# A planned attention-and-MLP kernel: lock rules for the port of VectorE and GpSimd, and a fourth quad with twenty VectorE tiles

## The chip, the cores and the metric

The kernel runs on one core of a Trainium2 chip. A core has TensorE (PE, matrix products), ScalarE (ACT, the exponential), VectorE (DVE), GpSimd (POOL) and a sync engine (SP) that issues DMAs. Each engine works through its own list of instructions in order; semaphores hold one engine back for another. Matrix products land in PSUM, eight banks of 128 x 512 float32; everything else lies in SBUF. The metric is device time in microseconds (us) for one execution, as the median over runs.

## The reference

One sequence of 2048 rows, width 512, in bfloat16. Attention with 32 heads of 16 channels, and a bilinear MLP with 1376 hidden channels, both on the same input, are mixed by a gate of each row:

```python
def _A_ref(x, wqkv, wo):                 # H = 32, Dh = 16
    qkv = (x @ wqkv).reshape(B, S, 3, H, Dh).transpose(2, 0, 3, 1, 4)
    q, k, v = qkv[0], qkv[1], qkv[2]
    scores = jnp.einsum("bhqd,bhkd->bhqk", q, k) * (Dh ** -0.5)
    p = softmax(scores, axis=-1)
    o = jnp.einsum("bhqk,bhkd->bhqd", p, v)
    return o.transpose(0, 2, 1, 3).reshape(B, S, D) @ wo
...
    h = jnp.einsum("bsd,df->bsf", x, w_gate) * jnp.einsum("bsd,df->bsf", x, w_up)
    b = jnp.einsum("bsf,fd->bsd", h, w_down)
...
x = A_x
g = sigmoid((x * gate_w).sum(-1, keepdims=True))
return g * a + (1 - g) * b
```

There are 32 heads x 2048 x 2048 scores, and each needs an exponential.

## The kernel before

**Tiles and quads.** Queries are cut into four chunks of 512. A *quad* is one chunk and four heads; there are 8 quads in a chunk and 32 in all, numbered m = 0 to 31. A *tile* is 128 keys by 512 queries of one head, so a quad has 16 key blocks x 4 heads = 64 tiles. TensorE makes a tile's scores with 32 of its rows, so up to four tiles of a quad are made at once (line 488, one step of `run_scores`).

**Two ways to the exponential.** Most tiles go to ScalarE: one instruction of `act_step` (line 1689) takes two or three neighbouring PSUM banks and writes bfloat16 into as many *cells* (512 columns of SBUF; most are in `PT`, others in `wv`, `hT` and `wd` while these are free). The other tiles, *D tiles*, go to VectorE (line 1076), which adds a constant to the scaled score, clips and stores it as a 16-bit integer that is read as bfloat16. This rough exponential is refined by averaging: three further copies of it with 32, 64 and 96 added (lines 1154 on VectorE, 1157 on GpSimd, made by `try_copy`, two tiles or on VectorE sometimes four at a time) are multiplied with weighted copies of V (`VD`, made on GpSimd at line 704; `VE`, line 718). A ScalarE tile thus needs one product with V, a D tile four (line 1219, `do_pv`, all into the bank psO).

**The split.** In an ordinary quad 48 tiles go to ScalarE and 16 to VectorE. For the quads in `HBQ` four more are D tiles (`xd`, with the key blocks in `XU`), 44 and 20. The extra ones need the small copies in `VE`, made for each block of 8 heads that occurs in `HBQ`. After a quad, psO is copied to SBUF (line 1248), reciprocals of the sums go through DRAM (SP's DMAs), and GpSimd multiplies (line 1280).

**Banks.** Six PSUM banks (psS) form two slots of three for scores. The first two of a slot always take ScalarE tiles; the third takes a ScalarE tile or a D tile. A seventh, psX, takes D tiles and *fills*: everything that is not attention (projections of Q, K and V, the MLP's up, gate and down products, the output product), as groups of up to 11 packs of four matmuls. VectorE evicts each fill. A Q fill is evicted to `qtmp` (line 622) and from there copied twice with a mask into `QM` (line 632), SBUF to SBUF.

**The planner.** The order on every engine is written by a simulation in `_build` that runs when the program is built. It keeps a clock for each engine, and steps the engine whose clock is lowest. Each task has a planned duration (`occ`) and a priority; `gen_step` picks for VectorE and GpSimd, `pe_step` and `filler` for TensorE, `act_step` for ScalarE. A fill has a position, in ScalarE tiles issued (`st["ua"]`), from which on it may run; `F0`, `F1`, `HWF` and `warp` set the positions of the MLP's fills. Only the order and the semaphores go into the program; on the chip an engine goes as fast as it is let.

**The lock.** [...] The plan keeps `lock["dve"]` and `lock["pool"]`, the times until which each holds it. GpSimd takes nothing before `lock["dve"]`; VectorE takes no weight copy (`try_copy`) before `lock["pool"]`; and a GpSimd task gets as dependency the VectorE task in front of the last weight copy (`lock["op"]`), so that the copy gets to the port first. The Q copies of line 632 are planned with 0.22 us and are outside of this rule:

```python
            if eng == "pool" and t < lock["dve"]:
                clock[eng] = lock["dve"]
                return True
```

Of the kernel before, what the change touches and what calls it, by code (L numbers as in the profile page):

```python
# [112 lines left out]

class _Task:

    __slots__ = ("eng", "deps", "fn", "occ", "lat", "prio", "cb", "stream", "dma", "op", "start", "end", "alloc", "pre")

    def __init__(self, eng, deps, fn, occ, lat=None, prio=5, cb=None, stream=None, dma=False, alloc=None):
        self.eng = eng
        self.deps = [d for d in deps if d is not None]  # L120
        self.fn = fn
        self.occ = occ
        self.lat = occ + 0.13 if lat is None else lat
        self.prio = prio
        self.cb = cb
        self.stream = stream
        self.dma = dma
        self.op = None
        self.start = None
        self.end = None  # L130
        self.alloc = alloc
        self.pre = None


class _Cell:
# [61 lines left out]
def _build(nc, A_x, A_wqkv, A_wo, W_gate, W_up, W_down, gate_w, out):  # L197
# [18 lines left out]
    NM = NQ * NCH  # L216
    RA = 24
    VW = 18
    HBQ = [16, 24, 30]
    HB = sorted({(m % NQ) // 2 for m in HBQ})  # L220
    XU = {1: 3, 4: 2, 7: 1, 10: 0}
    XI = {1: 0, 4: 1, 7: 2, 10: 3}
# [12 lines left out]
    with ExitStack() as stack:  # L235
# [243 lines left out]
            return old  # L479

        PACK = 0.2135
        PLAT = 0.44
        SW = 0.11
        pe = {"mode": "c"}
# [119 lines left out]
        def f_q(c, b, pos):  # L604
            packs = [
                (
                    lambda bk, kt=kt: col(
                        bk.ap, wq[:, kt, b * 128 : (b + 1) * 128], xT[:, kt, c * 512 : (c + 1) * 512], kt == 0, kt == KD - 1
                    ),
                    PACK,  # L610
                    "c",
                )
                for kt in range(KD)
            ]

            def evac(bk, last):
                if QT and (c or b):
                    bk.need += 1
                    e0 = add(
                        "dve",  # L620
                        [last] + qt_last,
                        lambda v: v.tensor_single_scalar(qtmp[:], bk.ap, QS, ALU.mult),
                        0.6,
                        prio=2,
                        cb=lambda k: bk.readers.append(k),
                    )
                    qt_last.clear()
                    for p in range(2):
                        ev_q[c, b, p] = add(
                            "dve",  # L630
                            [e0, o_mask] + q_last.get((c - 1, b), []),
                            lambda v, p=p: v.tensor_scalar(QM[:, p, b, :], qtmp[:], mask[:, p : p + 1], None, ALU.mult),
                            0.22,
                            prio=3.2,
                        )
                        qt_last.append(ev_q[c, b, p])
                    return
                bk.need += 2
                for p in range(2):
                    ev_q[c, b, p] = add(  # L640
                        "dve",
                        [last, o_mask] + q_last.get((c - 1, b), []),
                        lambda v, p=p: v.tensor_scalar(QM[:, p, b, :], bk.ap, mask[:, p : p + 1], QS, ALU.mult, ALU.mult),
                        0.66,
                        prio=2,
                        cb=lambda k: bk.readers.append(k),
                    )

            def deps():
                if c and not q_done.get((c - 1, b)):  # L650
                    return [None]
                return [d_wq[b]] + xdep(c)

            return Fill(f"q{c}{b}", packs, deps, evac, pos)
# [445 lines left out]
        def try_copy(eng, t):  # L1100
            best = None
            if eng == "pool" and dve_busy(t) < PB:
                return None
            for i, pr in enumerate(pairs):
                if not pr["k"] or not full(pr):
                    continue
                r = max(k.end for k in pr["p1"]) + (0.0 if eng == "dve" else SEM)
                if r > t:
                    continue
                if eng == "pool":  # L1110
                    k = pr["k"][-1]
                    if k < PK:
                        continue
                else:
                    k = pr["k"][0]
                    if k == 3 and r + (0.5 if st["ua"] >= NA - 12 else KW) > t:
                        continue
                best = (pr, k)
                break
            if best is None:  # L1120
                return None
            pr, k = best
            prs_ = [pr]
            if eng == "dve" and M4 and len(pr["u"]) == 2:
                for p2 in pairs[i + 1 : i + 4]:
                    if k in p2["k"] and full(p2) and len(p2["u"]) == 2 and max(x.end for x in p2["p1"]) <= t:
                        if even(pr["cell"] + p2["cell"]):
                            c = alloc(4, t)
                            if c is not None:
                                prs_.append(p2)  # L1130
                                break
            us = [(p_, x) for p_ in prs_ for x in range(len(p_["u"]))]
            n = len(us)
            c = alloc(max(n, 2), t)
            if c is None:
                return None
            c = c[:n]
            old = claim(c, 1)
            for p_ in prs_:
                p_["k"].remove(k)  # L1140
                if not p_["k"]:
                    pairs.remove(p_)
            if n == 4:
                _build.m4 += 1

            def cb(tk):
                for i, (p_, x) in enumerate(us):
                    cells[p_["cell"][x]].readers.append(tk)
                    add_tile(*p_["u"][x], k, c[i], tk)

            I16 = mybir.dt.int16
            src = tuple(p_["cell"][x] for p_, x in us)
            if eng == "dve":
                fn = lambda v: v.tensor_single_scalar(cell_ap(c, I16), cell_ap(src, I16), 32.0 * k, ALU.add)  # L1154
                occ = DCP + 0.133 * n
            else:
                fn = lambda g: g.tensor_scalar(cell_ap(c, I16), cell_ap(src, I16), 32.0 * k, 1.0, ALU.add, ALU.mult)  # L1157
                occ = PCP + 0.435 * n
            return _Task(eng, [x for p_ in prs_ for x in p_["p1"]] + old, fn, occ, cb=cb)
# [151 lines left out]
        QO = [0, 3, 1, 4, 2, 5, 6, 7]  # L1311
        fills = [q0[i] for i in QO] + q0[8:]
        wts = []
        HWF = 0.3
        GP = 200.0
        K3L = 190
        K3H = 260
# [9 lines left out]
        F0 = 210.0  # L1327
        WP = 36.0
        WL = 18.0
        F1 = 1490.0  # L1330
        fills.append(f_gate(GP))
        HW = 44.0 * HWF

# [103 lines left out]
        PB = 0.45  # L1437
        PK = 2
        KW = 4.0
        LAP = 0.1  # L1440
        LAC = 0.1
        CPR = 3.5
        LC = 6
        LDO = 8
        MG = 0.15
        FLATE = 12
# [4 lines left out]
        LA1 = 1  # L1451
        LA2 = 99
        XF = -99
        FB = 2
        SWE = 0
        NFD = 18
        AOH = 0.057
        M4 = 1
        _build.m4 = 0
# [1 line left out]
        PCP = 0.14  # L1461
        DEV = 0.6
        RSV = 0.5
        NP = 8
        KP = 1
        FBL = 15

        def a_idx():
# [231 lines left out]
        def gen_step(eng):  # L1700
            t = clock[eng]
            best = None
            if eng == "pool" and t < lock["dve"]:
                clock[eng] = lock["dve"]
                return True
            for k in qs[eng]:
                if best is not None and k.prio >= best.prio:
                    continue
                r = ready(k)
                if r is not None and r <= t:  # L1710
                    if k.alloc is not None:
                        old = k.alloc(t)
                        if old is None:
                            WHY.append((t, "p1cell"))
                            continue
                        k.deps = k.deps + old
                        k.alloc = None
                    best = k
# [4 lines left out]
            if eng in ("dve", "pool") and (best is None or best.prio > CPR):  # L1723
                if eng == "pool" or lock["pool"] <= t:
                    c = try_copy(eng, t)
                    if c is not None:
                        if eng == "dve":
                            lock["op"] = lock["prev"]
                            lock["prev"] = c
                        elif lock["op"] is not None:  # L1730
                            c.deps.append(lock["op"])
                        run_task(c, t)
                        lock[eng] = clock[eng]
                        return True
            if best is None:
                return False
# [1 line left out]
            if eng == "pool" and lock["op"] is not None:  # L1738
                best.deps.append(lock["op"])
            run_task(best, t)  # L1740
            if eng == "dve":
                lock["prev"] = best
            if eng == "pool":
                lock["pool"] = clock["pool"]
            return True

        o_woz = add(
# [208 lines left out]
```

The softmax here doesn't subtract the row's maximum and nothing guards it: scores larger than these inputs give would overflow.

## Time and profile before

| | |
|---|---|
| median of 3 runs | 714.72 us (714.56 to 714.99) |
| profiled execution, its own time | 714.88 us |
| span in that profile | 713.1 us |
| granted TensorE clock | 1.00 |
| first exponential starts, last one starts | 9.13 us, 702.74 us |
| instructions on line 1689 | 674 |

The page gives the busy time of each engine as a share of the span. A group row names line, engine, operation, output and input with shapes, the count, then busy time, mean duration in ns, and the idle time of the engine just before, with what ended it. In the order of time a row gives start, duration and count. ScalarE's instructions overlap in the records: a following one starts before the recorded end of the one before it, so durations are longer than the distance from start to start.

### The profile page before, as it was taken

To read this page: it belongs to the slowest core of one execution; us is meant where nothing else is said; L and a number is where in the kernel's file an instruction comes from. 1 tells how busy PE (TensorE), PEld (TensorE's weight loads), DVE (VectorE), ACT (ScalarE), POOL (GpSimd) and SP (SyncE) were. 2 spreads that over 40 slices of the span, in tenths; PEclk is the share of its full clock that TensorE was granted. 3 is DMA by queue.
4 is the path that set the end of the run, shared out by engine and by line. 5 is a ranking of instruction groups with operands and counts; after the bars stand their busy time and mean duration, and the time that the engine had idled before them with its cause. 6 is when DMAs were issued, how large, how long until landed. Compare 5 with 4: busy or idle time off the path is not lost. (4 is left out here: it accounts for less than half of the span.)

```text
span 713.1 us, 21304 instructions
## 1 busy us (share of the span) xinstructions
PE 688.0 (96%) x9115; PEld 188.2 (26%) x9115; DVE 643.2 (90%) x1229; ACT 699.1 (98%) x689; POOL 439.2 (62%) x463
## 2 busy tenths in 40 slices
PE   8999999999999999999999999999999999999997
PEld 3323232222222222222222222222222222222222
DVE  5999989999999888899988888999889988999887
ACT  6999999999999999999999999999999999999995
POOL 4648676565656566576577566655557676555682
PEclk9999999999999999999999999999999999999999
DMA  7700001000200001000000010000000000000001
GB/s 142 255 12 9 21 18 19 19 17 22 81 20 18 17 16 32 26 17 17 20 3 28 17 44 25 18 13 10 21 18 17 18 28 29 17 21 18 3 20 46
DMA packets 33055, 21.65 MB, mean 30 GB/s; under 512 B 20381, under 2 KB 27965, under 8 KB 32961
## 3 DMA queue, kind: packets, MB, share of 16 engines
q1 hardware_dynamic: 31632, 19.64, 9.2%
q8 instruction: 71, 1.16, 0.7%
q10 hardware_dynamic: 1328, 0.66, 0.4%
q14 instruction: 24, 0.19, 0.1%
HBM read 15.12 MB, written 2.36 MB: 25 GB/s over the span
## 5 line engine op out<-in xcount | busy, mean ns | idle before, releaser
L1689 ACT ACTIVATE PT<-psS 128x1024 bf16<-128x1024 f32 (+1 forms) x577 | 625.9, 1420 | 0.7 <-PE psS L488 0.6
L1157 POOL TENSOR_SCALAR PT<-PT 128x1024 int16<-128x1024 int16 x220 | 237.0, 1086 | 146.1 <-DVE PT L1154 38.9
L488 PE MATMUL psS<-QM,KE 32*128 32x512 bf16 x1968 | 255.2, 376 | 12.3 <-ACT PT L1689 6.6
L1076 DVE TENSOR_SCALAR PT<-psS 128x512 int16<-128x512 f32 x328 | 221.8, 685 | 23.9 <-PE psS L488 20.2
L1219 PE MATMUL psO<-PT,VS 128*18 128x512 bf16 x1709 | 227.7, 381 | 0.7 <-DVE oraw L1248 0.6
L1219 PE MATMUL psO<-PT,VD 128*18 128x512 bf16 x1231 | 192.3, 381 | 0.1
L1017 PEld LDWEIGHTS <-KE 32*128 32x128 bf16 x2048 | 63.1, 91 | 279.4 <-issue 166.4
L1154 DVE TENSOR_SCALAR PT<-PT 128x1024 int16<-128x1024 int16 (+1 forms) x232 | 101.4, 466 | 2.1 <-PE psO L1219 0.8
L1157 POOL TENSOR_SCALAR PT<-wv 128x1024 int16<-128x1024 int16 x57 | 61.0, 1078 | 40.9 <-DVE wv L1076 16.5
L1219 PEld LDWEIGHTS psO<-PT,VS 128*18 128x18 bf16 x1709 | 52.2, 88 | 59.8 <-issue 42.4
L1689 ACT ACTIVATE wv<-psS 128x1024 bf16<-128x1024 f32 (+1 forms) x47 | 60.3, 1311 | 0.0
L557 PE MATMUL psX<-wd,hT 128*32 128x512 bf16 (+1 forms) x704 | 59.0, 386 | 0.3 <-DVE wk L867 0.3
L1076 DVE TENSOR_SCALAR wv<-psS 128x512 int16<-128x512 f32 x76 | 51.8, 686 | 6.8 <-PE psS L488 6.3
L1219 PEld LDWEIGHTS psO<-PT,VD 128*18 128x18 bf16 x1231 | 45.3, 88 | 36.4 <-issue 22.9
L557 PE MATMUL psX<-xT,wu 128*32 128x512 bf16 x688 | 53.2, 383 | 1.0 <-DVE wv L1076 0.7
L557 PE MATMUL psX<-xT,wg 128*32 128x512 bf16 x688 | 52.5, 383 | 1.0 <-DVE PT L1076 0.7
L1219 PE MATMUL psO<-wv,VS 128*18 128x512 bf16 x182 | 49.9, 381 | 0.5 <-DVE oraw L1248 0.5
L1076 DVE TENSOR_SCALAR PT<-psX 128x512 int16<-128x512 f32 x58 | 39.8, 686 | 6.6 <-PE psS L488 6.4
L1689 ACT ACTIVATE wd<-psS 128x1024 bf16<-128x1024 f32 (+1 forms) x35 | 42.0, 1289 | 0.0
L1219 PE MATMUL psO<-wv,VD 128*18 128x512 bf16 x167 | 38.2, 381 | 0.0
L1157 POOL TENSOR_SCALAR wv<-PT 128x1024 int16<-128x1024 int16 x24 | 25.6, 1068 | 20.3 <-PE psO L1219 10.0
L830 DVE TENSOR_TENSOR hT<-psX,usb 128x512 bf16<-128x512 f32 (+1 forms) x44 | 30.0, 682 | 4.4 <-PE psX L557 4.3
(127 smaller groups left out, 704.0 us busy)
## 6 DMA issues: line engine op xcount, KB each, us to landing
rb<-rscr SPq DMA_DIRECT2D x31, 256.0 KB
out_dram<-ost SPq DMA_DIRECT2D x12, 128.0 KB, 1.7
wu<-in_B_w_up_dram SPq DMA_DIRECT2D x1, 1376.0 KB, 10.1
wg<-in_B_w_gate_dram SPq DMA_DIRECT2D x1, 1376.0 KB, 13.0
wd<-in_B_w_down_dram SPq DMA_DIRECT2D x1, 1280.0 KB, 6.1
OT<-OX SPq DMA_DIRECT2D x60, 16.0 KB, 1.8
wo<-in_A_wo_dram SPq DMA_DIRECT2D x1, 512.0 KB, 13.0
out_dram<-wk SPq DMA_DIRECT2D x4, 128.0 KB, 1.7
```

Source lines behind the costliest of these rows:

```text
L488: return e.add_instruction(mybir.InstMatmult(name=nc.get_next_instruction_name(), engine=mybir.EngineType.PE, ins=[e.lower_ap(rhs), e.lowe ...
L557: return e.matmul(out_ap[32 * q : 32 * q + w, :], lhs[:, 32 * q : 32 * q + w], rhs, start=s0, stop=s1, tile_position=(0, 32 * q), skip_gro ...
L830: lambda v: v.tensor_tensor(hT[0:w, f, :], bk.ap[0:w, :], usb[0:w, n % 2, :], ALU.mult),
L1017: r = e.ldweights(w, tile_position=pos)
L1076: lambda v: v.tensor_scalar(cell_ap(pr["cell"][i : i + 1], mybir.dt.int16), bk.ap, CB, 0.0, ALU.add, ALU.max),
L1154: fn = lambda v: v.tensor_single_scalar(cell_ap(c, I16), cell_ap(src, I16), 32.0 * k, ALU.add)
L1157: fn = lambda g: g.tensor_scalar(cell_ap(c, I16), cell_ap(src, I16), 32.0 * k, 1.0, ALU.add, ALU.mult)
L1219: r = e.matmul(psO[32 * j : 32 * j + VW, :], pv_stationary(m, kt, j, k), cell_ap((cell,)), start=s0, stop=s1, tile_position=(0, 32 * j), s ...
L1689: lambda a: a.activation(cell_ap(c), src, ACT.Exp, scale=LN2 / 128.0),
```

## The change

- `HBQ` becomes [16, 22, 24, 30]: quad 22 also gets 20 D tiles and 44 ScalarE tiles. The set of head blocks with `VE` copies stays {0, 3}.
- Tasks get a flag `x4`; the Q copies of line 632 carry it, and their planned duration goes from 0.22 to 0.26 us. A flagged task is not taken while GpSimd holds the port; taking it sets VectorE's lock and `lock["op"]`. GpSimd takes nothing while VectorE is within 0.3 us (`QMW`) of being free with a flagged task ready by then.
- GpSimd may start 0.07 us before the end of VectorE's lock (`LKD`); GpSimd's lock ends 0.1 us before its planned end (`LKP`).
- `try_copy` asks for a reserve of free cells (`RSC`) for copies of a quad later than the one whose products with V are running: two for each copy still owed to tiles up to the running quad. The reserve that the eviction of a D tile asks for is cut to three quarters (`KP`).
- Positions of the MLP's fills: `HWF` 0.3 to 0.2, `F1` 1490 to 1460. Their end goes from 1438.4 + 3 x 13.2 = 1478 to 1408.8 + 4 x 8.8 = 1444.
- Planner's numbers: `LAP` 0.1 to 0.12 (how long VectorE waits for a D tile that is about to be ready), `LC` 6 to 7 (how far D tiles may lag before one is converted to ScalarE), `FB` 2 to 0 (fills may start up to the time of the next scores), `NFD` 18 to 20 (free cells below which products with V go before a down product).

```diff
@@
-    __slots__ = (..., "alloc", "pre")
+    __slots__ = (..., "alloc", "pre", "x4")
...
-    HBQ = [16, 24, 30]
+    HBQ = [16, 22, 24, 30]
...
         PACK = 0.2135
+        QMC = 0.26
+        LKD = -0.07
+        LKP = 0.1
+        QMP = 3.2
+        QMW = 0.3
...
                             lambda v, p=p: v.tensor_scalar(QM[:, p, b, :], qtmp[:], mask[:, p : p + 1], None, ALU.mult),
-                            0.22,
-                            prio=3.2,
+                            QMC,
+                            prio=QMP,
+                            x4=True,
                         )
...
-            c = alloc(max(n, 2), t)
+            c = alloc(max(n, 2), t, False, RSC * sum(len(x["k"]) for x in pairs if x["u"][0][0] <= pvst["m"]) if pr["u"][0][0] > pvst["m"] else 0)
...
-        HWF = 0.3
+        HWF = 0.2
...
-        F1 = 1490.0
+        F1 = 1460.0
...
-        LAP = 0.1
+        LAP = 0.12
...
-        LC = 6
+        LC = 7
...
-        FB = 2
+        FB = 0
...
-        NFD = 18
+        NFD = 20
...
+        RSC = 1.0
...
-        KP = 1
+        KP = 0.75
...
-            if eng == "pool" and t < lock["dve"]:
-                clock[eng] = lock["dve"]
+            if eng == "pool" and t < lock["dve"] + LKD:
+                clock[eng] = lock["dve"] + LKD
+                return True
+            if eng == "pool" and QMW and clock["dve"] <= t + QMW and any(k.x4 and (ready(k) or 1e9) <= t + QMW for k in qs["dve"]):
+                clock[eng] += 0.05
                 return True
...
                 r = ready(k)
                 if r is not None and r <= t:
+                    if k.x4 and lock["pool"] > t:
+                        continue
...
                         run_task(c, t)
-                        lock[eng] = clock[eng]
+                        lock[eng] = clock[eng] - (LKP if eng == "pool" else 0.0)
...
             run_task(best, t)
-            if eng == "dve":
+            if eng == "pool":
+                lock["pool"] = clock["pool"] - LKP
+            elif eng == "dve":
+                if best.x4:
+                    lock["dve"] = clock["dve"]
+                    lock["op"] = lock["prev"]
                 lock["prev"] = best
-            if eng == "pool":
-                lock["pool"] = clock["pool"]
             return True
```

More of the change, by code (lines that the diff above doesn't have):

```diff
@@ L114, with __init__ @@
 class _Task:
-    __slots__ = ("eng", "deps", "fn", "occ", "lat", "prio", "cb", "stream", "dma", "op", "start", "end", "alloc", "pre")
-    def __init__(self, eng, deps, fn, occ, lat=None, prio=5, cb=None, stream=None, dma=False, alloc=None):
+    __slots__ = ("eng", "deps", "fn", "occ", "lat", "prio", "cb", "stream", "dma", "op", "start", "end", "alloc", "pre", "x4")
+    def __init__(self, eng, deps, fn, occ, lat=None, prio=5, cb=None, stream=None, dma=False, alloc=None, x4=False):
         self.eng = eng
@@ L132, in __init__ @@
         self.pre = None
+        self.x4 = x4
 class _Cell:
```

## The prediction

> **What bounds the kernel now.** I read the busy shares first.
>
> ```profile
> span 713.1 us, 21304 instructions
> PE 688.0 (96%) x9115; PEld 188.2 (26%) x9115; DVE 643.2 (90%) x1229; ACT 699.1 (98%) x689; POOL 439.2 (62%) x463
> ```
>
> ScalarE and TensorE are both nearly full, so the shares do not decide between them. The order of time does: the first exponential (line 1689) starts at 9.13 us, the last one starts at 702.74, and ScalarE's idle rows between them add up to under 1 us. TensorE has 25 us of visible idle time, spread out. ScalarE therefore sets the time, and the next view is its groups, each shape apart (busy time, mean ns of one, idle before).
>
> ```profile
> L1689 ACT ACTIVATE PT<-psS 128x1024 bf16<-128x1024 f32 x406 | 435.7, 1297 | 0.1
> L1689 ACT ACTIVATE PT<-psS 128x1536 bf16<-128x1536 f32 x170 | 287.5, 1718 | 0.7 <-PE psS L488 0.6
> L1689 ACT ACTIVATE wv<-psS 128x1024 bf16<-128x1024 f32 x45 | 56.9, 1295 | 0.0
> L1689 ACT ACTIVATE wd<-psS 128x1024 bf16<-128x1024 f32 x30 | 35.1, 1234 | 0.0
> L1689 ACT ACTIVATE hT<-psS 128x1024 bf16<-128x1024 f32 x15 | 16.8, 1230 | 0.2 <-PE psS L488 0.2
> L1689 ACT ACTIVATE wd<-psS 128x1536 bf16<-128x1536 f32 x5 | 8.1, 1619 | 0.0
> L1689 ACT ACTIVATE wv<-psS 128x1536 bf16<-128x1536 f32 x2 | 3.3, 1665 | 0.0
> L1689 ACT ACTIVATE PT<-psS 128x512 bf16<-128x512 f32 x1 | 0.9, 895 | 0.0
> ```
>
> That is 496 instructions over two tiles, 177 over three, one over a single tile: 674 instructions, 1524 tiles, which is 32 quads x 48 less 3 x 4. No tile was converted to ScalarE on the way. Durations overlap by some 0.4 us, so they cannot be added; start-to-start times can. In the order of time a row of seven two-tile instructions starts at 40.97 and the next row at 47.39, 6.42/7 = 0.917 us each. Over the whole trace, with the late starts left out, two tiles take 0.910 us and three take 1.336 us, so a tile costs 0.426 and an instruction 0.058, as the planner has it (0.4267 and 0.057). The work is then 496 x 0.910 + 177 x 1.337 = 688.0 us, out of 702.74 - 9.13 = 693.6. About 5.5 us are lost, and by start times 4.9 of them lie in 25 late starts of over 20 ns. They do not show as idle time because the overlap swallows the first 0.4 us of each. The sum of the profiled execution is 9.1 (head) + 688.0 + 5.6 (late starts and rounding) + 10.4 (from the last start to the end) = 713.1 us span. That execution took 714.88 us, 1.8 around the span; the median of the runs is 714.72.
>
> **Where the late starts come from.** The longest one is 0.86 us at 450.23. Its neighbourhood in order of time (start, duration, engine, line):
>
> ```profile
> 446.16 2.08 POOL L1157 TENSOR_SCALAR PT<-PT 128x1024 int16<-128x1024 int16 x2
> 446.76 1.63 DVE L632 TENSOR_SCALAR QM<-qtmp,mask 128x512 bf16<-128x512 bf16 x2
> ...
> 448.31 0.67 DVE L1076 TENSOR_SCALAR wv<-psX 128x512 int16<-128x512 f32 x1
> ...
> 449.04 0.83 PE L557 MATMUL psX<-xT,wu 128*32 128x512 bf16 x12 [0.73 <-DVE wv L1076]
> ...
> 449.80 0.39 PE L488 MATMUL psS<-QM,KE 32*128 32x512 bf16 x3
> ...
> 450.23 1.45 ACT L1689 ACTIVATE PT<-psS 128x1536 bf16<-128x1536 f32 x1 [0.41 <-PE psS L488]
> ```
>
> Two masked Q copies (line 632) overlap two GpSimd copies and take 1.63 us. Alone the pair takes 0.60:
>
> ```profile
> 38.14 0.60 DVE L632 TENSOR_SCALAR QM<-qtmp,mask 128x512 bf16<-128x512 bf16 x2
> ```
>
> The eviction of bank X behind them comes a microsecond late, TensorE waits 0.73 us with a fill for that bank, the scores stand behind the fill in TensorE's order, and the exponential misses its start. Of the 30 Q copies, 9 take over 0.08 us more than the 0.345 of a free one, 5.1 us in all. Taking every late start with such a Q copy in the 4.5 us before it: 62.96, 83.21, 84.29, 139.3, 182.18, 313.65, 450.23 and 486.98, together 2.88 us of the 4.95. Three more (229.63, 237.95, 651.06), 0.81 us, follow a weight copy (line 1154) that lost a whole GpSimd instruction, 0.88 us; one at 14.79 (0.21) and a part of 62.96 have one near too. The remaining 0.9 us are single starts of 0.02 to 0.12 us.
>
> **The change part by part.**
>
> Fourth heavy quad (HBQ gets 22). Four tiles go from ScalarE to VectorE. ScalarE: 4 x 0.4267 = 1.71 us less, if the instruction count stays. It should: a step's own third bank goes to a third ScalarE tile or to a VectorE tile. Of the 524 VectorE tiles 444 sit in psS and 80 in psX (line 1076 by output and input), 177 third banks went to ScalarE, so 674 - 177 - 444 = 53 were unused. With N steps, 2N + (N - 444 - 53) = 1524 gives N = 673.7. With 528 VectorE tiles, 448 in psS and 1520 on ScalarE, N is again (1520 + 501)/3 = 673.7. If 20 tiles more or fewer fit into psX, N moves by 7. The price of an instruction is where a rule and the trace part: the Trainium skill, "ScalarE: Activation LUTs" (section "ACT is a hardware spline evaluator"), gives 186 ns plus 0.833 ns an element with 93 ns of overlap back to back, so 93 ns fixed. By that the 674 instructions would take 674 x 0.093 + 1524 x 0.4267 = 713 us, more than the 693.6 there are; I take the trace's 0.058. Seven instructions are 0.4 us by the row, 0.65 by the rule. They stay in the range.
>
> VectorE gets 4 evictions x 0.60 (start to start) = 2.4 us and its share of 6 pair copies, at most 6 x 0.42 = 2.5; it has 70 us idle. TensorE gets 12 PV matmuls, three packs of 0.2135 = 0.64 us. No weighted V copies are added on GpSimd, since quad 22 uses block 3, as quad 30 does. What would hurt is TensorE, and the heavy quads of now show how near that is (by stretch: length, PE, PEld, DVE, ACT, POOL busy; quads 16, 24, 30):
>
> ```profile
> 358.60:379.00 20.40, 20.39 (x257) 4.90 (x249) 17.04 (x34) 20.40 (x23) 14.60 (x15) 1.00 0.04 9
> 531.60:551.60 20.00, 19.89 (x241) 4.57 (x241) 17.71 (x33) 20.00 (x22) 14.87 (x15) 1.00 0.05 15
> 660.80:680.80 20.00, 19.93 (x244) 4.58 (x245) 18.16 (x37) 20.00 (x22) 12.12 (x13) 1.00 0.04 11
> ```
>
> TensorE is over 99% busy there and ScalarE still never idles; the late starts in these 60 us come to 0.08. A fourth such quad I cost at 0 beyond its tiles. If that cover were gone, the 0.64 us would fall on ScalarE.
>
> Q copies as port users (x4, QMC, QMW). They now wait in the plan until GpSimd's pair is free, later GpSimd work waits for the VectorE instruction before them, and GpSimd holds back while one is due within 0.3 us. QMC 0.26 is what the trace has between two free copies (0.60 - 0.34). I take back 80% of the 2.88 us, 2.3: the order of issue is fixed, but drift can still let GpSimd win a race, as it did against weight copies that were already planned this way. Bounds: 0 to 2.9. GpSimd pays: 15 pairs x (0.3 + 0.6) = 13.5 us at most, out of 274 idle. Behind the waiting instruction on its queue stand weight copies and the normalisation (line 1280), whose reader is a quad, some 21 us, away; VectorE takes over at most a dozen pair copies at 0.42 = 5 us. Both are hidden.
>
> Release times (LKD -0.07, LKP 0.1). Here a rule speaks against the change: the Trainium skill, "SBUF — State Buffer" (section "SBUF: two separate sides"), says that whichever starts first gets the shared pair for the whole instruction. By it a VectorE copy planned 0.1 us before GpSimd's end only blocks: at most 350 copies x 0.1 = 35 us of VectorE's 70 idle, and new lateness. The trace disagrees on the end: the second pair instruction of GpSimd above starts at 447.17, the Q copy behind it ends at 448.39 (446.76 + 1.63) and needs 0.34, so the pair was free at about 448.05, 0.88 after the start. The plan said 1.01, and now says 0.91: still on the safe side. Worth between 0 and the 1.0 us of weight-copy lateness; I take 0. LKD costs GpSimd at most 350 x 0.07 = 25 us, in its idle time.
>
> The rest (cell reserve RSC, KP, NFD, LC, FB, LAP, fill positions HWF and F1). They reorder, and add no instruction. ScalarE waits for no cell now, and conversions are zero, so RSC, KP and LC have nothing to gain on that path. Fill positions end 34 tiles (15 us) sooner and each quarter is 2.4% shorter, 307 to 300 tiles: of the 29 packs that a normal quad has room for, 0.7 more, 0.15 us in 22. The output DMAs on SP's queue, four of 128 KB a quarter, move with them; the DMA engines are 4 to 9% busy there. I take 0, between -0.9 (all remaining small late starts gone) and +1.0 (ten new ones of about 0.1). The tail after the last start stays at 10.4, +-0.4.
>
> Sum: 714.7 - 1.7 - 2.3 = **710.7 us**.
>
> **Rivals.** (a) The ports are not mended: drift moves the lost races elsewhere, only the tiles count: 714.7 - 1.7 = 713.0. For it: weight copies were planned with a lock and still lost 11 us in 34 places. Against it: not one Q copy had that protection. 16%. (b) Weight copies win as well and the small late starts shrink: 714.7 - 1.7 - 2.9 - 1.0 - 0.4 = 708.7. For it: the release figures fit the trace. Against it: they are three races among 419 copies. 12%. (c) Slower: the cell reserve holds back the copies of the next quad, so each quad's PV work begins short of tiles; TensorE runs out of filler there and ScalarE misses a start at each of the 31 quad changes. At 0.25 us each that is 7.8, so 714.7 - 4.0 + 7.8 = 718.5; it eats the gain from 4.0/31 = 0.13 us per change on. For it: PV's weight loads already wait for the evicted accumulator at quad changes, 6.5 us in 9 places. Against it: scores and fills stand ready as filler, and those waits reach no late start. 7%.
>
> **How the numbers follow.** Forecast 65%, its own range 709.3 to 712.2. With the rivals, 708.4 to 713.6 leaves out about half of (b)'s lower side, part of (a) and all of (c). A measurement tells 0.2%, 1.4 us, from no change: faster means under 713.3. Forecast, (b) and six tenths of (a) lie there, 0.86; within 0.2% the rest of (a), 0.07; slower (c), 0.07.
>
> **What would show it.** 1520 tiles in about 674 instructions, 528 evictions on line 1076; Q copies all near 0.35 us; late starts down from 4.9 to about 2.6 us, the first start near 9.1, the last start 10.4 before the end. It would be wrong if instructions rise well over 680, if late starts move to weight copies or fills, or if ScalarE waits for TensorE at quad changes.

## The result and the profile after

The changed kernel takes 712.08 us (median of 4 runs, 711.77 to 712.38) against 714.83 (714.56 to 714.99): a ratio of 0.9962, 95% interval 0.9945 to 0.9979. That is 2.75 us less where 4.0 were forecast, and 1.4 us above the forecast's 710.7. The profiled execution took 711.77 us, with a span of 710.0.

Busy shares of the changed kernel, from its page:

```profile
span 710.0 us, 21364 instructions
...
PE 688.3 (97%) x9127; PEld 188.7 (27%) x9127; DVE 644.5 (91%) x1231; ACT 696.6 (98%) x686; POOL 459.3 (65%) x481
```

TensorE has the 12 more matmuls that the fourth quad adds, GpSimd does 18 more pair copies, ScalarE has three instructions fewer. Its groups on the exponential (now line 1697), each shape apart:

```profile
L1697 ACT ACTIVATE PT<-psS 128x1024 bf16<-128x1024 f32 x405 | 444.8, 1343 | 0.1
L1697 ACT ACTIVATE PT<-psS 128x1536 bf16<-128x1536 f32 x163 | 285.4, 1775 | 0.0
L1697 ACT ACTIVATE wv<-psS 128x1024 bf16<-128x1024 f32 x43 | 58.1, 1352 | 0.0
L1697 ACT ACTIVATE wd<-psS 128x1024 bf16<-128x1024 f32 x28 | 33.8, 1295 | 0.0
L1697 ACT ACTIVATE hT<-psS 128x1024 bf16<-128x1024 f32 x15 | 17.5, 1251 | 0.2 <-PE psS L494 0.2
L1697 ACT ACTIVATE wd<-psS 128x1536 bf16<-128x1536 f32 x9 | 15.9, 1772 | 0.0
L1697 ACT ACTIVATE wv<-psS 128x1536 bf16<-128x1536 f32 x5 | 8.8, 1763 | 0.0
L1697 ACT ACTIVATE hT<-psS 128x1536 bf16<-128x1536 f32 x2 | 3.6, 1777 | 0.0
L1697 ACT ACTIVATE PT<-psS 128x512 bf16<-128x512 f32 x1 | 0.9, 932 | 0.0
```

491 over two tiles, 179 over three and one single make 671 instructions and 1520 tiles. One thing looks odd: the durations have grown, from 1297 to 1343 ns for the largest group, while the kernel got faster. This is the key to the sizes, and the next section comes back to it.

The Q copies in the group view, first of the kernel before (line 632), then of the changed one:

```profile
L632 DVE TENSOR_SCALAR QM<-qtmp,mask 128x512 bf16<-128x512 bf16 x30 | 14.3, 515 | 0.1
```

```profile
L638 DVE TENSOR_SCALAR QM<-qtmp,mask 128x512 bf16<-128x512 bf16 x30 | 10.4, 381 | 0.1
```

The longest takes 0.75 us where it was 1.17. Four of the 30 still take over 0.08 us more than a free one, 1.2 us in sum, where it was nine and 5.1; no late start follows them. The pair of Q copies in front of the longest late start, the twelfth of 15, has its counterpart here, in order of time:

```profile
438.54 1.08 POOL L1164 TENSOR_SCALAR PT<-PT 128x1024 int16<-128x1024 int16 x1 [1.17 <-DVE wv L1161]
...
439.38 0.69 DVE L1083 TENSOR_SCALAR PT<-psS 128x512 int16<-128x512 f32 x1
439.59 0.37 PE L494 MATMUL psS<-QM,KE 32*128 32x512 bf16 x3
439.89 1.05 PE L563 MATMUL psX<-xT,wg 128*32 128x512 bf16 x16
439.99 0.61 DVE L638 TENSOR_SCALAR QM<-qtmp,mask 128x512 bf16<-128x512 bf16 x2
440.87 0.39 PE L494 MATMUL psS<-QM,KE 32*128 32x512 bf16 x3
```

GpSimd's copy is over at 439.62, before the Q copies begin at 439.99; they take 0.61, and the fill and the scores run on without a wait.

**The account by ends.** ScalarE's instructions overlap in the records, so a late start does not tell how much later the work is done. The distance from one instruction's end to the next one's does. With two tiles an end follows the last one after 916.6 ns, with three after 1343.4, and this hardly varies: from the 5th to the 95th percentile it is 915 to 918 and 1342 to 1345 in both kernels. A tile costs 0.427 and an instruction 0.063 us. What exceeds these steps by over 0.03 us I count as lost by ends.

| us | before | after | difference |
|---|---|---|---|
| first exponential ends | 10.16 | 9.81 | -0.35 |
| the steps of all others | 691.9 | 690.0 | -1.9 |
| lost by ends, and rounding | 1.6 | 0.4 | -1.2 |
| from the last end to the end of the span | 9.46 | 9.79 | +0.34 |
| span | 713.1 | 710.0 | -3.1 |

Of the 1.9 us, 1.7 are the four tiles and 0.2 the three instructions. The places where time was lost went from eight (1.47 us) to two (0.25). The first line of the table differs between executions, so its 0.35 us is no gain of the change: the first exponential starts anywhere from 8.66 to 9.49 us over the fourteen profiles of this case.

### The profile page after: what moved, and what is told of

It is laid out like the page before. It is cut to its first block, busy times and chain, and to the rows that moved or that the text cites. A ratio compares the mean times of both kernels' runs of the same rounds, so it can differ in the third digit from the quotient of the medians.

```text
span 710.0 us, 21364 instructions
## 1 busy us (share of the span) xinstructions
PE 688.3 (97%) x9127; PEld 188.7 (27%) x9127; DVE 644.5 (91%) x1231; ACT 696.6 (98%) x686; POOL 459.3 (65%) x481
## 4 chain that ended last, share of the span: by engine, by line
ACT 70%; PE 22%; DVE 3%; issue 3%; POOL 1%; DVEq 0%; POOLq 0%; ACTq 0%
ACT PT L1697 59%; PE psS L494 8%; PE psO L1226 6%; PE psX L563 5%; ACT wd L1697 5%; ACT wv L1697 4%; ACT hT L1697 2%; DVE PT L1083 1%; PE psS L563 1%; POOL PT L1164 1%; DVE PT L1161 1%; PE psX L494 1%; PE psO L1805 0%; DVE wk L898 0%; PE psS L1816 0%
## 5 line engine op out<-in xcount | busy, mean ns | idle before, releaser
L1164 POOL TENSOR_SCALAR PT<-PT 128x1024 int16<-128x1024 int16 x233 | 250.5, 1084 | 134.9 <-DVE PT L1161 46.3
L1083 DVE TENSOR_SCALAR PT<-psS 128x512 int16<-128x512 f32 x349 | 237.2, 686 | 26.9 <-PE psS L494 24.0
L1226 PE MATMUL psO<-PT,VS 128*18 128x512 bf16 x1698 | 225.3, 381 | 1.0 <-DVE oraw L1255 1.0
L1226 PE MATMUL psO<-PT,VD 128*18 128x512 bf16 x1228 | 194.9, 381 | 0.0
L1697 ACT ACTIVATE wv<-psS 128x1024 bf16<-128x1024 f32 (+1 forms) x48 | 67.0, 1395 | 0.0
L1083 DVE TENSOR_SCALAR wv<-psS 128x512 int16<-128x512 f32 x71 | 48.3, 687 | 7.0 <-PE psS L494 6.7
L1226 PE MATMUL psO<-wv,VS 128*18 128x512 bf16 x179 | 51.4, 381 | 0.0
L1697 ACT ACTIVATE wd<-psS 128x1024 bf16<-128x1024 f32 (+1 forms) x37 | 47.6, 1411 | 0.0
L1083 DVE TENSOR_SCALAR PT<-psX 128x512 int16<-128x512 f32 x49 | 33.7, 688 | 5.7 <-PE psS L494 5.1
```

The costliest lines, as they stand in the source:

```text
L1083: lambda v: v.tensor_scalar(cell_ap(pr["cell"][i : i + 1], mybir.dt.int16), bk.ap, CB, 0.0, ALU.add, ALU.max),
L1226: r = e.matmul(psO[32 * j : 32 * j + VW, :], pv_stationary(m, kt, j, k), cell_ap((cell,)), start=s0, stop=s1, tile_position=(0, 32 * j), s ...
L1697: lambda a: a.activation(cell_ap(c), src, ACT.Exp, scale=LN2 / 128.0),
```

## Experiments

All times are medians; each ratio is to the kernel before on the same chip at the same time, with its 95% interval. Differences between two runs are of medians; the kernel before stayed between 714.51 and 714.83 beside them. One table first. Its last five columns are from the profiles: "tiles" and "instructions" are ScalarE's exponentials, "last down" is the end of the last matmul of the MLP's down product, "tail" the time from the end of ScalarE's last exponential to the end of the span.

| kernel | time | ratio | tiles | instructions | lost by ends | last down | tail |
|---|---|---|---|---|---|---|---|
| before | 714.8 | 1 | 1524 | 674 | 1.5 | 691.9 | 9.5 |
| after | 712.08 | 0.9962 (0.9945 to 0.9979) | 1520 | 671 | 0.2 | 691.5 | 9.8 |
| e1 before, quad 22 | 723.25 | 1.0119 (1.0104 to 1.0134) | 1520 | 688 | 2.4 | 715.1 | 17.7 |
| e2 after, three quads | 714.08 | 0.9991 (0.9984 to 0.9997) | 1524 | 667 | 0.5 | 683.7 | 9.4 |
| e3 after, Q copies unlocked | 717.55 | 1.0037 (1.0023 to 1.0052) | 1520 | 683 | 0.6 | 707.9 | 14.0 |
| e4 before, lock rules | 713.51 | 0.9984 (0.9977 to 0.9990) | 1524 | 668 | 0.7 | 685.7 | 9.2 |
| e5 after, old numbers | 715.69 | 1.0012 (1.0005 to 1.0019) | 1520 | 677 | 1.0 | 706.0 | 12.8 |
| e6 after, old positions | 715.69 | 1.0015 (1.0007 to 1.0024) | 1520 | 671 | 0.4 | 703.7 | 13.2 |
| e7 after, scores 0.21 late | 712.16 | 0.9962 (0.9947 to 0.9976) | 1520 | 671 | 0.5 | 691.7 | 9.8 |
| e8 after, scores 0.64 late | 716.58 | 1.0023 (1.0015 to 1.0032) | 1520 | 671 | 4.4 | 696.1 | 9.8 |
| e9 after, no early release | 721.98 | 1.0101 (1.0084 to 1.0118) | 1520 | 692 | 1.0 | 712.5 | 17.9 |
| e10 after, other seed | 711.83 | 0.9958 (0.9944 to 0.9973) | 1520 | 668 | 1.5 | 683.9 | 9.2 |
| e11 after, five quads | 719.99 | 1.0074 (1.0059 to 1.0089) | 1516 | 690 | 1.2 | 710.2 | 17.7 |
| e12 after, six old numbers, new positions | 715.02 | 1.0007 (0.9998 to 1.0016) | 1520 | 671 | 2.5 | 697.6 | 11.5 |

### Is a late start lost?

**e7** and **e8** leave the plan alone and multiply 14 steps of scores two and four times instead of once, with the same values into the same banks, so that they are late:

```diff
+            slow = len(RUNS) in range(80, 640, 40)
...
-                for u, bk in us:
-                    w, x, pos = loc(u)
-                    r = mm(e, bk.ap, w, x, pos)
+                for _ in range(1 + 1 if slow else 1):      # e8: 3 + 1
+                    for u, bk in us:
+                        w, x, pos = loc(u)
+                        r = mm(e, bk.ap, w, x, pos)
```

> The changed kernel in which 14 steps of scores, every 40th from the 80th on, are multiplied twice (same values into the same banks), so that each is some 0.21 us late on TensorE; order and plan unchanged, the additional work is only there to be late. Theory of the prediction (a late start of ScalarE is lost in full): up to 14 x 0.21 = 3.0 us, 714 to 715. Theory of the ends (a start may come some 0.34 us late for nothing): under 0.5 us, 712.1 to 712.6, with 1 to 3 us more of late starts in sum but not by ends.

> The same 14 steps multiplied four times, so that each is some 0.64 us late. Theory of the prediction: up to 14 x 0.64 = 9 us, 718 to 721. Theory of the ends: the first 0.34 us of each are absorbed, and what TensorE has of idle time before it: 14 x 0.3 = 4.2 us at most, 713 to 716.3.

14 steps 0.21 us late cost nothing that the runs can tell, where 3.0 us were due if a late start is lost in full: the ratio is that of the changed kernel to the fourth digit, while the late starts in sum went from 1.8 to 4.4 us, so the lateness did reach ScalarE. 14 steps 0.64 us late cost 716.58 - 712.08 = 4.5 us, 0.32 each: the other 0.32 was absorbed. The stretch from 100 to 640 us, which holds 13 of the 14 places (length, then PE, PEld, DVE, ACT, POOL busy), first of the changed kernel:

```profile
100.00:640.00 540.00, 527.57 (x6853) 138.68 (x6849) 496.79 (x943) 540.00 (x523) 345.87 (x323) 1.00 0.08 22
```

and of e8:

```profile
100.00:640.00 540.00, 529.22 (x6917) 137.39 (x6795) 491.38 (x935) 537.61 (x520) 343.84 (x320) 1.00 0.07 22
```

ScalarE does three instructions fewer and 2.4 us of it show as idle. One place of e8, the last instruction of the stream and the late one, each alone:

```profile
257.23 1.37 ACT L1699 ACTIVATE PT<-psS 128x1024 bf16<-128x1024 f32 x1
258.79 1.02 ACT L1699 ACTIVATE PT<-psS 128x1024 bf16<-128x1024 f32 x1 [0.20 <-PE psS L494]
```

The first row ends at 258.59. The next instruction starts 0.20 later and, coming to an empty engine, takes only 1.02 us, so its end is 1.22 after the last instead of 0.917: 0.30 lost. In the stream the same instruction shows 1.36 to 1.37 us, so some 0.34 of that is waiting behind the one in front. This waiting is what a late start uses up first. It is also why durations grew in the changed kernel: its instructions are on time more often. With the lateness put in, the mean of the largest group falls again, from 1343 ns to 1298 in e7, at the same time, and to 1242 in e8. The theory of the prediction, that a late start is lost in full, falls.

### What the four tiles and the lock rules do alone and together

**e1** is the kernel before with the fourth quad:

```diff
-    HBQ = [16, 24, 30]
+    HBQ = [16, 22, 24, 30]
```

> The kernel before with HBQ = [16, 22, 24, 30] and nothing else. Both theories give the tiles 4 x 0.427 = 1.7 us: about 713.1 against 714.8, 1520 tiles in some 672 to 676 instructions. Q copies still lose races to GpSimd (several near 1.1 us), and by the ends of ScalarE's instructions 1 to 2 us are still lost. Rival (the tiles bring nothing since TensorE is full in a heavy quad): 714.8.

8.4 us slower, which neither expectation had. ScalarE's part is as expected, 691.1 us of steps with the last exponential ending at 703.9, but the kernel goes on for 17.7 us. What ScalarE waited for after its last exponential, first e1, then the changed kernel:

```profile
ACT oraw L1906 <- PE psS L557: 9.4, 1, 9.4
```

```profile
ACT oraw L1922 <- PE psS L563: 2.5, 1, 2.5
```

In e1 the matmuls of the MLP are not done. The last down products, in order of time, of e1, then of the changed kernel:

```profile
713.85 1.25 PE L557 MATMUL psX<-wd,hT 128*32 128x512 bf16 x20
```

```profile
690.88 0.62 PE L563 MATMUL psX<-wd,hT 128*32 128x512 bf16 x8
```

Where they fell behind shows in the stretch from 520 to 640 us, after quad 22, of e1 and of the changed kernel (columns as above):

```profile
520.00:640.00 120.00, 118.10 (x1453) 28.72 (x1457) 107.39 (x206) 120.00 (x125) 77.97 (x72) 1.00 0.07 21
```

```profile
520.00:640.00 120.00, 117.24 (x1511) 30.15 (x1511) 111.13 (x208) 120.00 (x118) 83.95 (x78) 1.00 0.07 22
```

TensorE is as busy in e1, but gets through 58 matmuls fewer (over the whole program both traces hold 9127), and ScalarE does 125 instructions instead of 118. More instructions for the same tiles are more steps with two ScalarE tiles. A step costs TensorE more than a pack of 0.2135. In the changed kernel, in order of time:

```profile
437.33 0.37 PE L494 MATMUL psS<-QM,KE 32*128 32x512 bf16 x3
437.63 1.05 PE L563 MATMUL psX<-xT,wq 128*32 128x512 bf16 x16
438.61 0.39 PE L494 MATMUL psS<-QM,KE 32*128 32x512 bf16 x3
```

The scores take 0.30; the four packs behind them take 0.98 where 4 x 0.2135 is 0.85; so a step costs 0.43. Over all steps of this trace, in median, the pack behind starts 0.305 after the scores and the scores 0.325 after the pack in front, where a pack follows a pack in 0.216 to 0.22: 0.41. The plan counts 0.2135 and twice 0.11 (`SW`), 0.43. 17 steps more than in the changed kernel are 7.3 us of TensorE, and the tail is 7.9 longer. The sum comes out alike in three more runs: e3 12 steps, 5.2 us, tail +4.2; e9 21, 9.0, +8.1; e11 19 steps and 0.6 for its PV packs, 8.8, +7.9. It is not the only way to a longer tail: e6 and e12, below, have no step more than the changed kernel and a tail 3.4 and 1.7 us longer.

**e4** is the lock rules alone on the kernel before (the changed kernel with `HBQ = [16, 24, 30]` and the old eight numbers):

> The lock rules alone on the kernel before: x4, QMC, QMW, LKD and LKP as changed; three heavy quads, RSC 0, KP 1, and the old fill positions and planner numbers. Theory of the prediction: 714.8 - 2.3 to 2.9 = about 712.2. Theory of the ends: 714.8 - 1.0 to 1.3 = about 713.7, late starts down from 4.9 to about 2 us, lost by ends under 0.5 us.

1.3 us faster, what the ends gave and not the prediction's 2.3 or more. No late start follows a blocked Q copy, 0.7 us are lost by ends instead of 1.5, and six instructions are saved. The release times are part of it; the rule for the Q copies was not run alone.

**e2** is the changed kernel with `HBQ = [16, 24, 30]`:

> The changed kernel with HBQ back to [16, 24, 30], nothing else. If tiles and ports add up: 712.1 + 1.7 = 713.8, 1524 tiles, Q copies all short, under 0.6 us lost by ends. If the ports were the whole gain: 712.1.

714.08: by the medians the fourth quad is worth 2.0 us there. Eight of e2's 20 executions had a granted clock of 0.993 to 0.996; the other twelve, at 0.998 or more as all four of the changed kernel, have a median of 713.46, and by that it is 1.4. The tiles' 1.7 lies between. Whether the other eight numbers cost anything with three heavy quads is not shown: e2 is 0.6 us above e4 by all its executions and level with it (713.46 against 713.51) by those twelve. The tiles thus bring about their 1.7 us or cost 8.4, depending on the rest.

### What carries the fourth quad

**e3** takes the flag from the Q copies:

```diff
-        QMC = 0.26
+        QMC = 0.22
...
-                            x4=True,
```

> The changed kernel with the flag x4 off and the Q copies planned at 0.22 us as before; the release times, the fourth quad and all other numbers stay. Theory of the prediction (a late start is lost in full, 2.9 us of them behind Q copies): 712.1 + 2.3 to 2.9 = 714.4 to 715.0. Theory of the ends (ScalarE's overlap of some 0.34 us absorbs the first part of a late start; by ends only 1.0 us was lost behind Q copies before): 713.1, with late starts of 2 to 3 us in sum and 0.7 to 1.5 us lost by ends.

717.55, above both expectations, and not for the reason that either had: by ends only 0.6 us are lost, though 12 Q copies were blocked again for 4.9 us in sum. The plan with this rule left out makes 683 steps, the fills end 16 us later and the tail is 14.0.

**e9** leaves out the early releases:

```diff
-        LKD = -0.07
-        LKP = 0.1
+        LKD = 0.0
+        LKP = 0.0
```

> The changed kernel with LKD and LKP at 0 (GpSimd's lock ends with its planned end, VectorE's with its own), all else as changed. Theory of the prediction: worth 0 to 1.0 us, 712.1 to 713.1. Theory B (what the lock rules do to the plan counts, not the waits that they spare on the chip: with 0.1 us lost at each hand-over VectorE is late for bank X, more steps with two ScalarE tiles are made, and TensorE's fills fall behind): over 680 instructions on line 1689's successor, last down product after 700 us, tail over 12 us, 715 to 722.

721.98, as theory B has it: 692 steps, last down product 712.5, tail 17.9. These two numbers, which the prediction cost at nothing, carry 9.9 us in the changed kernel. My reading is that a tenth of a microsecond at each hand-over is time of VectorE in the plan. The split of the D tiles fits it: 418 of 528 D tiles were read from psS, and with 137 three-tile instructions among 692 steps that leaves 692 - 137 - 418 = 137 third banks unused; in the changed kernel it is 671 - 179 - 461 = 31.

**e6** has the old fill positions, **e5** all eight old numbers, **e12** the old six with the new positions. The diff is that of e6:

```diff
-        HWF = 0.2
-        F1 = 1460.0
+        HWF = 0.3
+        F1 = 1490.0
```

> The changed kernel with HWF 0.3 and F1 1490 as before, all else as changed. Theory B with the positions as the part that counts: last down product later than 691.5 by up to 15 us, tail longer by 2 to 8 us, 714 to 720. If the positions don't count: 712.1 and the same tail.

> The lock rules and the fourth quad, but the eight planner numbers as before (HWF 0.3, F1 1490, LAP 0.1, LC 6, FB 2, NFD 18, RSC 0, KP 1). Theory A (lock and quad are what counts, the numbers are worth nothing): 712.1, tail after the last exponential 9.8 us. Theory B (with a fourth heavy quad TensorE and bank X can only just carry the fills; the numbers, fill positions above all, keep them on time): the last down product ends several us after the 691.5 of the changed kernel, the tail grows to 12 to 17 us, 714 to 719.

> The changed kernel with LAP 0.1, LC 6, FB 2, NFD 18, RSC 0 and KP 1 as before; lock rules, fourth quad and the new fill positions stay. If the positions are all that the fourth quad needs beside the lock rules: 712.1, tail 9.8 us. If the other six numbers carry a part: the last down product some us after 691.5 and a tail of 11 us or more, 713.5 to 716.

e6 is 3.6 us slower with ScalarE's part unchanged (671 instructions, 690.0 us): nearly all of it is tail, 13.2 against 9.8. The fills' positions end 34 tiles later, and the last down product follows 12 us later. e5 is as slow; its tail of 12.8 is no longer than that of e6, so its six extra steps add nothing to what the positions do. e12 is 2.9 slower, with 1.7 of longer tail and 2.2 more lost by ends, 1.1 of it in two starts, at 541.98 and 544.72 us, and 1.0 in one at 22.17. So the positions and the other six carry about 3 us each when put back alone, and no more than that together.

**e11** has a fifth quad, `HBQ = [14, 16, 22, 24, 30]`:

> The changed kernel with a fifth heavy quad, HBQ = [14, 16, 22, 24, 30], all else as changed. If ScalarE alone bounds: 712.1 - 1.7 = 710.4. Theory B (TensorE and bank X are the second bound, and four quads use what there is): the last down product after 700 us, a tail of 13 us or more, 715 to 720.

719.99. ScalarE's last exponential ends at 700.5, and the tail is 17.7: four quads are what this plan carries.

**e10** changes only `SEED = 2` to 5:

> The changed kernel with SEED 5 in place of 2, which shifts each fill's position by another 0 to 6 tiles and gives another order with the same rules. If the gain comes from the rules and numbers: 712.1 within 0.7. If it is the luck of one order: a time between that of before and the changed kernel, or above.

711.83, so the gain is not the luck of one order. It did not beat the changed kernel by more than the two vary: its interval covers the other.

**Is the longer tail made on the chip or in the plan?** The order is fixed when the program is built, and the traces hold TensorE's order. Behind the last scores stand 116 matmuls of the down product in e1 (29 packs, 6.2 us at 0.2135), 136 in e9, 140 in e11, 76 in e3, 44 in e5 and 24 in e6. In all other kernels, before and changed among them, it is none; e12, with a tail 1.7 us longer, has 16 matmuls with V more there than the changed kernel. On the chip TensorE has time to spare: e7 gives it 14 x 0.215 = 3.0 us more work in the order of the changed kernel, and the last down product (691.7) and the tail (9.8) stay. So the tail is made in the plan, which leaves fills to the end.

Not settled: whether the planner leaves the fills behind for want of TensorE's time, at 0.43 us a step, or of bank psX, which extra D tiles and late evictions hold longer. TensorE fits better: the D tiles in psX are 67 in the changed kernel, 99 in e1, 90 in e3, 110 in e9 and 82 in e11, and e11 has the tail of e1. A run that loads one in the plan and not the other was not made. Why the Q rule changes the plan's number of steps was not traced either.

## Why the prediction was right, and where it was not

The 712.08 lies in the forecast's range, 709.3 to 712.2, by 0.12 us, and nearer to rival (a)'s 713.0 than to 710.7. So the number alone would not have told the two apart; the experiments do.

**ScalarE sets the time**: right for the two kernels compared, and only as long as the fills end before the last exponential. The tail, taken as 10.4 us from the last start within 0.4, did stay, 10.4 before and 10.7 after, but as a condition and not as a constant: it ran from 9.2 to 17.9 in these runs (from the last end).

**Four tiles, 1.71 us**: right, 1.7 of the 1.9 by ends and 1.4 to 2.0 in e2 against the changed kernel. "A fourth such quad I cost at 0 beyond its tiles" holds for the whole change alone. If the cover were gone, I wrote, 0.64 us would fall on ScalarE. e1 shows it gone: the cost does not fall on ScalarE but on the end, and it is 8 us, since its plan has 14 steps more than the kernel before.

**The instruction count stays**: it came to 671 for 674. But it rested on 53 unused third banks, and this number is no constant: 31 after, 137 in e9. The price of an instruction, 0.058 us from starts, is 0.063 by ends; that is still below the 93 ns of the rule that I set beside it.

**The ports, 2.3 us**: mechanism right, size wrong. All late starts behind Q copies are gone, and the late starts went from 4.9 to 1.8 us, further down than the 2.6 forecast. But "about 5.5 us are lost" was the failed step: it took starts for work. After a late start the next ones come closer together (0.904 us apart in e8 from 261.04 on, where ends come every 0.917), so the 0.910 with the late starts left out was too small a price, and 688.0 too small a sum. By ends 1.5 us were lost, 1.0 of it at four of the places named (84.29, 139.3, 313.65, 450.23), and 1.2 came back in all. This term made the forecast too large by 1.1 us. With 1.9 + 1.2 in place of 1.7 + 2.3, and a head and tail that cancel, the profiled executions differ by 3.1 us; the medians differ by 2.75.

**Release times at 0, the rest at 0 between -0.9 and +1.0**: wrong as parts. In the changed kernel the release times carry 9.9 us, the positions and the other six numbers about 3 each. I asked what each spares on the chip, and for numbers of a planner the question is what order comes out. The blocking that the quoted rule for the pair threatened, up to 35 us of VectorE, did not come: VectorE's two-tile weight copies lost 11.0 us in 33 places before (counted from 0.08 us over the median of 0.42), 15.1 in 52 after, and 12.5 in 40 without the release times (e9). The sum came out near because the changed plan, as a whole, keeps the fills on time, which I had assumed and not derived.

**Rivals.** (a) does not hold: the lock rules without the fourth quad gain 1.3 us (e4). (b) does not hold: the time is 3.4 us above its 708.7, and the weight copies are held up more than before, not less. (c), the cell reserve, did not occur: by ends nothing is lost to a wait at a quad change in the changed kernel. Its two places are the starts at 14.44 and 126.98 us, and in front of the second ScalarE does a short instruction for the gate (126.88), not a wait. A slower case was close by, but another one: a plan in which the fills fall behind. Five of the partial versions here (e1, e3, e5, e6, e9) end there, and e12 in part.

## What to carry to other kernels

Measure the bound engine by the ends of its instructions: here starts that came late within the overlap cost nothing. When work is moved off the engine that sets the time, look for the work that has to be finished by its last instruction; here the engine second in line did not slow the first, it lengthened the tail. And don't add up the edits of a planned order one by one: the same four tiles were worth under 2 us or cost 8, depending on whether the plan still had room for them.

## What the runs showed of the hardware

- ScalarE's exponential, read from PSUM and written in bfloat16: 916.6 ns for 1024 columns and 1343.4 for 1536 from end to end. The recorded start of an instruction lies up to 0.45 us before the recorded end of the one in front, and of 0.64 us of lateness 0.32 is absorbed without loss (e8).
- A pair of Q copies takes 0.60 us by itself and 1.63 where two GpSimd copies run beside it (446.76 in the kernel before), so one waits for the other. It is let through before GpSimd's record ends. In the changed kernel, in order of time:

```profile
111.01 2.05 POOL L1164 TENSOR_SCALAR wd<-wv 128x1024 int16<-128x1024 int16 x2
...
112.51 0.95 DVE L638 TENSOR_SCALAR QM<-qtmp,mask 128x512 bf16<-128x512 bf16 x2
```

The Q copies end at 113.46. If they need their 0.60 undisturbed, they went from 112.86 on, an estimate: 0.20 before GpSimd's row ends at 113.06. The kernel before has 0.19 (448.05 against 448.24).
